# A hedgehog-attention and MoE kernel on one core: the quads of attention run as a software pipeline, with the matrix instructions in program order, the two MoE products mixed, and the tail loads made per batch

## The chip, the cores and the metric

The kernel runs on one core of a Trainium2 chip. The metric is the device time of one execution in microseconds; lower is better. The engines that matter are TensorE (PE in the profile; its weight loads are PEld), VectorE (DVE), ScalarE (ACT) and GpSimd (POOL). The sync engine (SP) only issues DMAs here.

## The reference, cut to what matters

```python
def phi(x):                              # q, k, v: batch 8, heads 8, 576 rows, 64 wide
    proj = einsum('bhsd,df->bhsf', x, w_phi)              # w_phi: 64 x 128
    proj = proj - max(abs(proj), axis=-1)
    return concatenate([exp(proj), exp(-proj)], axis=-1)
q_p, k_p = phi(q), phi(k)
kv  = einsum('bhsf,bhsd->bhfd', k_p, v)
num = einsum('bhsf,bhfd->bhsd', q_p, kv)
den = einsum('bhsf,bhf->bhs', q_p, sum(k_p, axis=2)) + 1e-6
x = (num / den), heads side by side                       # 4608 tokens x 512
h = x @ moe_w_in                                          # 512 x 2048
g = where(h > 0, h, exp(min(h, 0)) - 1)
out = g @ moe_w_out                                       # 2048 x 512
```

## The kernel before, in words

The attention is done in 16 quads: quad i holds four heads of batch i // 2. Of each head's 576 rows, 512 are the main part (four tiles of 128) and 64 are a tail; the tails of the four heads share tiles of their own (k_tails, q_tails, v_tails). The MoE is done in nine chunks of 512 tokens: one for each batch's main rows, and a ninth for all tails together.

The steps of a quad, with the names that the profile shows:

- transposes: PE turns k_main and q_main (tile tr, 16 products) and the tails (trt, 2) around, DVE copies them to kT and qT.
- k_head, five times (four heads and the tails): PE projects into pk, DVE takes the largest absolute value into m_k (the reduction), and ACT writes two exponentials (EK, or EKt for the tails). The exponentials wait for the reduction, because both read one bank of PSUM.
- k_scale: ACT makes em from m_k, and POOL multiplies v by it: four pieces of vs and two of vst.
- q_head, five times: the projection and the reduction into m_q alone. q_features: PE projects q again into pq, four times 512 wide and once for the tails, and ACT writes two exponentials of each (Eq, Eqt), then w from m_q.
- kv, twice: PE sums pkv over EK and vs (16 products of 65 columns and two of 130), ACT copies it to kv.
- out_head, four times, and out_tail: PE makes pn0 and pn1 from Eq and kv, DVE combines them into tot with two instructions (the tails into tott with four).
- divide: DVE makes den and rec, POOL multiplies tot by rec into x (four pieces) and xt.
- x_out: PE turns x around (eight products into tr and one into trt), DVE copies it to xT and xT_tail, the MoE's input.

An MoE chunk is 20 units. A unit of mm1 is four products of 512 columns into ph; then ACT makes e_sb, POOL u_sb and DVE gT. It is run 16 times. A unit of mm2 is 16 products of 512 columns into po; ACT copies it to o_sb and SP sends it off. It is run four times and reads all 16 pieces of gT.

Both halves take their PSUM from pools of four banks: apsum for everything of the attention (tag ap), mpsum for ph and po (tag mp). A tile of a pool waits until the last reader of the tile that held its bank is done.

In the program the steps of one quad follow each other, and the units of the batch before are dealt out between them: half of a batch's 20 units with each of the next two quads. The last batch and the tails' chunk (40 units) come after the last quad. That order is only a proposal: the framework's scheduler sets the order of the instructions on each engine when the program is built, by priorities and its own estimate of times. On the chip each engine then works through its list in order.

All loads with a change of type (q, k, the weights, the tails) are issued from POOL's list, among its computing instructions; v and the output go over SP.

Of the kernel before, what the change touches and what calls it, by code (L numbers as in the profile page):

```python
# [21 lines left out]
def kernel(  # L22
# [10 lines left out]
    nc = tc.nc  # L33
    P = 128
# [42 lines left out]
    w_in_r = moe_w_in.rearrange("(ct p) j -> p ct j", p=P)  # L77
# [3 lines left out]
    def load_w_in():  # L81
        for ct in range(N_CT):
            nc.gpsimd.dma_start(out=w_in_sb[:, ct, :], in_=w_in_r[:, ct, :])
# [16 lines left out]
    def load_tails(g0, g1):  # L100
        for src, dst, eng in (
            (k, k_tails, nc.gpsimd),
            (q, q_tails, nc.gpsimd),
            (v, v_tails, nc.gpsimd),
        ):
            flat = src.rearrange("b (g h) s d -> (b g) h s d", g=2)
            for s in range(2):
                for c in range(2):
                    eng.dma_start(
                        out=dst[s * TAIL:(s + 1) * TAIL, g0:g1, c, 0:D],  # L110
                        in_=flat[g0:g1, 2 * s + c, MAIN:S, :].rearrange(
                            "g j d -> j g d"
                        ),
                    )
# [40 lines left out]
    def attention_steps(i):  # L155
# [93 lines left out]
        def q_features(par, s):  # L249
            pq = apsum.tile([P, 4 * P], FP32, name="pq", tag="ap")  # L250
            nc.tensor.matmul(  # L251
                pq,
                w_phi_both[:, par, :],
                st["qT"][:, 4 * s:4 * s + 4, :].rearrange("p a b -> p (a b)"),
                start=True,
                stop=True,
            )
            for sg in range(2):
                nc.scalar.activation(  # L259
                    st["Eq"][:, par, s, sg, :], pq, ACT.Exp, scale=1.0 - 2.0 * sg  # L260
                )
# [22 lines left out]
        def kv(c):  # L284
# [12 lines left out]
            for s in range(2):  # L297
                for sg in range(2):
                    for t in range(NT):
                        nc.tensor.matmul(  # L300
                            pkv[:, s, sg, :],
                            st["EK"][:, 2 * s + c, sg, t * F:(t + 1) * F],
                            st["vs"][:, 2 * s + c, sg, t, :],
# [6 lines left out]
        def out_head(hh):  # L310
            s, c = divmod(hh, 2)
# [6 lines left out]
            for sg in range(2):  # L318
                pt = apsum.tile([P, NT, D1], FP32, name=f"pn{sg}", tag="ap")
                for t in range(NT):  # L320
                    tp, par = divmod(t, 2)
                    o = (2 * c + tp) * P
                    nc.tensor.matmul(  # L323
                        pt[:, t, :],
                        st["Eq"][:, par, s, sg, o:o + P],
# [39 lines left out]
        def divide():  # L365
# [9 lines left out]
            for hh in range(4):  # L375
                s, c = divmod(hh, 2)
# [52 lines left out]

# [112 lines left out]
```

## Time and profile before

| | |
|---|---|
| device time, two runs | 571.85 and 575.05 us, median 573.45 |
| the profiled execution | 574.21 us, of which the profile spans 572.4 |
| mean granted clock of PE | 0.901 |
| busy share of the span | PE 73%, DVE 51%, ACT 46%, POOL 46% |

The profile is of one execution. Busy time counts an instruction from its start to its end. Matmuls overlap, so their ends lie over the next one's start, and the distance of two starts says more than one's duration. Behind each row of a timeline stands, in square brackets, how long the engine had been idle ahead of it and what ended that. Lines are those of the kernel before; in the kernel after, the same lines stand one lower or so (L230 is L229 there).

### The profile page before, as it was taken

Reading aid. Unit: us, or ns where it says so; the run is one execution under the profiler, and the core shown is the slowest. Engines: PE = TensorE matmul, PEld = TensorE weight load, DVE = VectorE, ACT = ScalarE, POOL = GpSimd, SP = SyncE. Lnnn points to the kernel's source line nnn. Section 1 sums busy time; section 2 is a strip of 40 time slices with the busy share of each in tenths; the row PEclk is TensorE's granted clock in tenths of the full one; section 3 lists DMA queues with packets and bytes.
Section 4 is the critical chain, followed back from the end, with each engine's and each line's share of the span. In section 5 each row is a group of like instructions: output and inputs, shape, how many; then the busy total and the mean of one; then the engine's idle time right before and its main releaser. Section 6 shows DMA issues by size and latency. Waiting matters only on the chain.

```text
span 572.4 us, 8389 instructions
## 1 busy us (share of the span) xinstructions
PE 416.2 (73%) x3066; PEld 232.1 (41%) x3120; DVE 292.0 (51%) x647; ACT 264.8 (46%) x581; POOL 263.3 (46%) x392
## 2 busy tenths in 40 slices
PE   2302557768866786868787896778768867789996
PEld 1102334434443443434344444444435434444443
DVE  2300646484548435763576466836484538527070
ACT  1600244654374518371836265635655373725251
POOL 7637234654365426551556236633644265426060
PEclk9855767799989799999988998999799979899999
DMA  9999312122312215041403231323100100010103
GB/s 161 194 198 137 47 38 37 38 38 73 74 38 38 50 54 82 1 74 57 84 10 57 73 57 38 42 70 74 38 0 35 42 1 2 19 56 1 74 1 73
DMA packets 71496, 32.55 MB, mean 57 GB/s; under 512 B 47904, under 2 KB 66336, under 8 KB 71456
## 3 DMA queue, kind: packets, MB, share of 16 engines
q0 software_dynamic: 32416, 14.19, 21.7%
q1 hardware_dynamic: 39040, 17.83, 11.8%
q8 instruction: 24, 0.39, 0.3%
q14 instruction: 16, 0.13, 0.1%
HBM read 36.77 MB, written 9.44 MB: 81 GB/s over the span
## 4 chain that ended last, share of the span: by engine, by line
PE 31%; POOL 26%; issue 16%; DVE 11%; ACT 9%; DMA 6%; POOLq 0%; ACTq 0%; DVEq 0%
POOL vs L230 11%; PE po L459 11%; PE ph L438 10%; POOL x L377 6%; ACT EK L216 6%; DVE gT L451 4%; POOL vst L241 3%; DMA w_out_sb<-in_moe_w_out_dram 3%; PE tr L167 3%; POOL u_sb L448 3%; DVE tot L332 2%; DVE tot L338 2%; PE pkv L300 2%; PE pk L196 2%; DMA w_in_sb<-in_moe_w_in_dram 2%
## 5 line engine op out<-in xcount | busy, mean ns | idle before, releaser
L438 PE MATMUL ph<-xT,w_in_sb 128*128 128x512 bf16 x482 | 136.1, 394 | 18.0 <-DVE gT L451 16.1
L448 POOL TENSOR_SCALAR u_sb<-e_sb 128x512 bf16<-128x512 f32 x144 | 88.1, 619 | 116.9 <-ACT e_sb L446 105.7
L451 DVE SCALAR_TENSOR_TENSOR gT<-u_sb,ph 128x512 bf16<-128x512 bf16 x144 | 95.7, 681 | 86.5 <-POOL u_sb L448 85.7
L459 PE MATMUL po<-w_out_sb,gT 128*128 128x512 bf16 x554 | 138.9, 389 | 0.8
L446 ACT ACTIVATE e_sb<-ph 128x512 f32<-128x512 f32 x144 | 89.6, 636 | 102.6 <-PE ph L438 79.1
L438 PEld LDWEIGHTS <-w_in_sb 128*128 128x128 bf16 x576 | 55.6, 101 | 68.2 <-issue 31.0
L230 POOL TENSOR_TENSOR vs<-v_main,em 128x520 bf16<-128x520 f32 x64 | 65.7, 1056 | 36.3 <-ACT em L224 36.3
L377 POOL TENSOR_TENSOR x<-tot,rec 128x256 bf16<-128x256 f32 x64 | 37.2, 614 | 92.1 <-DVE rec L374 91.0
L459 PEld LDWEIGHTS <-gT 128*128 128x128 bf16 x576 | 55.4, 100 | 57.9 <-issue 4.2
L216 ACT ACTIVATE EK<-pk 128x512 bf16<-128x512 f32 x128 | 64.6, 633 | 24.3 <-DVE m_k L203 24.3
L467 ACT COPY o_sb<-po 128x512 f32<-128x512 f32 x36 | 21.1, 586 | 114.4 <-PE po L459 114.4
L332 DVE TENSOR_TENSOR tot<-pn,w 128x260 f32<-128x260 f32 x64 | 24.9, 424 | 93.1 <-PE pn L323 92.8
L259 ACT ACTIVATE Eq<-pq 128x512 bf16<-128x512 f32 x128 | 67.6, 712 | 4.7 <-PE pq L251 4.7
L289 PE MATMUL pkv<-vst,EKt 128*128 128x130 bf16 x64 | 11.2, 271 | 72.8 <-POOL vst L241 52.7
L203 DVE TENSOR_REDUCE m_q<-pk 128x4 f32<-128x512 f32 (+1 forms) x80 | 48.4, 634 | 10.0 <-PE pk L196 9.0
L203 DVE TENSOR_REDUCE m_k<-pk 128x4 f32<-128x512 f32 (+1 forms) x80 | 46.4, 630 | 2.8 <-PE pk L196 2.5
L289 PEld LDWEIGHTS <-EKt 128*128 128x128 bf16 x64 | 6.7, 108 | 80.1 <-issue 69.6
L308 ACT CAST kv<-pkv 128x260 bf16<-128x260 f32 x32 | 12.0, 376 | 57.1 <-PE pkv L300 57.1
L196 PE MATMUL pk<-w_phi_both,qT 128*128 128x256 bf16 x144 | 28.1, 301 | 13.0 <-ACT EK L216 11.3
L394 PE MATMUL tr<-ident,x 128*128 128x128 bf16 x128 | 13.5, 232 | 24.9 <-POOL x L377 24.9
L401 DVE COPY xT<-tr 128x1024 bf16<-128x1024 bf16 x16 | 11.1, 692 | 39.2 <-PE tr L394 39.2
L196 PE MATMUL pk<-w_phi_both,kT 128*128 128x256 bf16 x144 | 25.0, 287 | 7.4 <-ACT EK L216 6.5
(61 smaller groups left out, 473.0 us busy)
## 6 DMA issues: line engine op xcount, KB each, us to landing
v_main<-in_v_dram SPq DMA_DIRECT2D x64, 128.0 KB, 2.6
out_dram<-o_sb SPq DMA_DIRECT2D x32, 256.0 KB, 2.3
k_main<-in_k_dram POOLq DMA_DIRECT2D x16, 256.0 KB, 4.4
q_main<-in_q_dram POOLq DMA_DIRECT2D x16, 256.0 KB, 4.9
w_in_sb<-in_moe_w_in_dram POOLq DMA_DIRECT2D x4, 512.0 KB, 9.6
w_out_sb<-in_moe_w_out_dram POOLq DMA_DIRECT2D x4, 512.0 KB, 17.3
out_dram<-o_sb SPq DMA_DIRECT2D x8, 128.0 KB, 2.3
k_tails<-in_k_dram POOLq DMA_DIRECT2D x4, 96.0 KB, 13.8
```

Of the source, the lines that this page charges most:

```text
L196: nc.tensor.matmul(pk[:, 2 * j:2 * j + 2, :].rearrange("p a b -> p (a b)"), xT[:, 2 * hh + j, :], w_phi_rhs, start=True, stop=True,)
L203: nc.vector.tensor_reduce(m[:, 4 * hh:4 * hh + 2 * n], pk[:, 0:2 * n, :], axis=AX.X, op=ALU.max, apply_absolute_value=True,)
L216: nc.scalar.activation(dst, pk, ACT.Exp, scale=1.0 - 2.0 * sg)
L230: nc.gpsimd.tensor_tensor(vs[:, hh], vb[:, hh:hh + 1].to_broadcast((P, 2, NT, D1)), em[:, :, 4 * hh:4 * hh + 4, None].to_broadcast((P, 2, ...
L259: nc.scalar.activation(st["Eq"][:, par, s, sg, :], pq, ACT.Exp, scale=1.0 - 2.0 * sg)
L332: nc.vector.tensor_tensor(tot, pn[1], st["w"][:, 4 * hh:4 * hh + 4, None].to_broadcast((P, NT, D1)), op=ALU.mult,)
L377: nc.gpsimd.tensor_tensor(st["x"][:, s, :, c, :], st["tot"][:, hh, :, 0:D], rec[:, 4 * hh:4 * hh + 4, None].to_broadcast((P, NT, D)), op=A ...
L438: nc.tensor.matmul(ph, w_in_sb[:, ct, jt * P:(jt + 1) * P], xTs[ch][:, ct, :], start=(ct == 0), stop=(ct == N_CT - 1),)
L446: nc.scalar.activation(e_sb, ph, ACT.Exp)
L448: nc.gpsimd.tensor_scalar(u_sb, e_sb, -1.0, 1.0, op0=ALU.add, op1=ALU.mult)
L451: nc.vector.scalar_tensor_tensor(gTs[ch][:, jt, :], u_sb, 0.0, ph, op0=ALU.min, op1=ALU.max)
L459: nc.tensor.matmul(po, gT[:, jt, tt * P:(tt + 1) * P], w_out_sb[:, jt, :], start=(jt == 0), stop=(jt == N_JT - 1),)
```

## The change

Seven things are done.

1. The program's order of steps is written in slots. Slot n holds the k steps, k_scale, the q steps and q_features of quad n, together with kv, out and x of quad n - 1; kv and out alternate with the k steps on PE. The transposes of quad n + 1 end the slot. There are 17 slots (0 to 16).
2. PE's instructions are held in program order; the scheduler still orders the other engines.
3. The units of MoE chunk c are mixed: after every fourth mm1 of chunk c stands one mm2 of chunk c - 1. Batch 0's chunk has no mm2 beside it, and four mm2 of the last chunk are left for the end.
4. The units are dealt out a slot later: 8 (all mm1) in each of the slots 3 and 4, 10 (eight mm1, two mm2) in each of the slots 5 to 16, none ahead. What stands behind slot 16 is 32 units of mm1 and 12 of mm2.
5. The tails of q, k and v are loaded per batch, with six DMAs of 64 x 4 runs each: one batch at the start, the next after every second slot. Before, there were 12 such DMAs for quads 0 to 3 and then 12 with three times as many runs for the rest.
6. w_out is loaded after slot 1 in the program, behind w_in; w_in comes in eight pieces of 64 partitions, not four of 128.
7. The heads of a quad are paired otherwise (c and s change places throughout, and the rows of w_in with them). The instructions and their sizes stay the same.

```diff
     w_phi_rhs = w_phi_both.rearrange("p a b -> p (a b)")
     w_in_sb = consts.tile([P, N_CT, DFF], BF16)
-    w_in_r = moe_w_in.rearrange("(ct p) j -> p ct j", p=P)
+    w_in_r = moe_w_in.rearrange("(g c s d) j -> g c s d j", g=2, c=2, s=2)
     w_out_sb = consts.tile([P, N_JT, DM], BF16)
     w_out_r = moe_w_out.rearrange("(jt p) o -> p jt o", p=P)
     def load_w_in():
         for ct in range(N_CT):
-            nc.gpsimd.dma_start(out=w_in_sb[:, ct, :], in_=w_in_r[:, ct, :])
+            for c in range(2):
+                nc.gpsimd.dma_start(
+                    out=w_in_sb[c * D:(c + 1) * D, ct, :],
+                    in_=w_in_r[ct // 2, c, ct % 2],
+                )
     def load_w_out():
         for jt in range(0, N_JT, 4):
@@ -97,21 +101,16 @@
     v_tails = consts.tile([P, NQ, 2, D1], BF16)
     nc.vector.memset(v_tails[:, :, :, D:D1], 1.0)
-    def load_tails(g0, g1):
-        for src, dst, eng in (
-            (k, k_tails, nc.gpsimd),
-            (q, q_tails, nc.gpsimd),
-            (v, v_tails, nc.gpsimd),
-        ):
-            flat = src.rearrange("b (g h) s d -> (b g) h s d", g=2)
+    def load_tails(b):
+        for src, dst in ((k, k_tails), (q, q_tails), (v, v_tails)):
+            heads = src[b].rearrange("(gc s) j d -> s j gc d", s=2)
             for s in range(2):
-                for c in range(2):
-                    eng.dma_start(
-                        out=dst[s * TAIL:(s + 1) * TAIL, g0:g1, c, 0:D],
-                        in_=flat[g0:g1, 2 * s + c, MAIN:S, :].rearrange(
-                            "g j d -> j g d"
-                        ),
-                    )
+                nc.gpsimd.dma_start(
+                    out=dst[s * TAIL:(s + 1) * TAIL, 2 * b:2 * b + 2, :, 0:D].rearrange(
+                        "p g c d -> p (g c) d"
+                    ),
+                    in_=heads[s, MAIN:S],
+                )
     NV = 3
@@ -246,18 +245,18 @@
                 )
             st["vs"], st["vst"] = vs, vst
-        def q_features(par, s):
+        def q_features(par, c):
             pq = apsum.tile([P, 4 * P], FP32, name="pq", tag="ap")
...
@@ -415,17 +414,18 @@
         def each(f, *a):
             return lambda: f(*a)
-        return (
-            [transposes]
-            + [each(k_head, hh) for hh in range(5)]
-            + [k_scale]
-            + [each(q_head, hh) for hh in range(5)]
-            + [each(q_features, par, s) for s in range(2) for par in range(2)]
-            + [q_features_tail]
-            + [each(kv, c) for c in range(2)]
-            + [each(out_head, hh) for hh in range(4)]
-            + [out_tail, divide, x_out]
-        )
+        return {
+            "tr": [transposes],
+            "k": [each(k_head, hh) for hh in range(5)],
+            "scale": [k_scale],
+            "q": [each(q_head, hh) for hh in range(5)],
+            "qf": [each(q_features, par, c) for c in range(2) for par in range(2)]
+            + [q_features_tail],
+            "kv": [each(kv, c) for c in range(2)],
+            "out": [each(out_head, hh) for hh in range(4)]
+            + [lambda: (out_tail(), divide())],
+            "x": [x_out],
+        }
     gTs = {}
@@ -476,39 +476,86 @@
                     in_=o_sb[e * TAIL:(e + 1) * TAIL, :],
                 )
-    def moe_units(ch):
-        return [lambda jt=jt: mm1(ch, jt) for jt in range(N_JT)] + [
-            lambda tt=tt: mm2(ch, tt) for tt in range(CHUNK // P)
-        ]
+    def slot_steps(n):
+        new = attention_steps(n) if n < NQ else None
+        old = quads.get(n - 1)
+        nxt = []
+        steps = []
+        k = new["k"] if new else [None] * 5
+        qs = new["q"] if new else [None] * 5
+        if old:
+            steps += [old["kv"][0], k[0], old["kv"][1], k[1]]
+            for hh in range(3):
+                steps += [old["out"][hh], k[2 + hh]]
+            steps += [old["out"][3], new and new["scale"][0], old["out"][4]]
+        else:
+            steps += k + new["scale"]
+        steps += qs
+        if old:
+            steps += old["x"]
+        if new:
+            steps += new["qf"]
+            quads[n] = new
+        if n + 1 < NQ:
+            steps.append(lambda: transpose_next(n + 1))
+        return [f for f in steps if f]
+    quads = {}
+    ready = {}
+    def transpose_next(n):
+        ready[n] = build_steps(n)
+        ready[n]["tr"][0]()
+    build_steps = attention_steps
+    def attention_steps(n):
+        return ready.pop(n)
+    def mixed_units(ch):
+        units = []
+        for jt in range(N_JT):
+            units.append(lambda jt=jt: mm1(ch, jt))
+            if ch > 0 and jt % 4 == 3:
+                units.append(lambda tt=jt // 4: mm2(ch - 1, tt))
+        return units
+    ctx.enter_context(tc.manual_schedule(engines={mybir.EngineType.PE}))
     load_quad(0)
-    load_tails(0, 4)
+    load_tails(0)
     load_quad(1)
     load_w_in()
     load_quad(2)
-    load_w_out()
-    load_tails(4, NQ)
+    transpose_next(0)
     pending = []
-    for i in range(NQ):
-        b, qd = divmod(i, 2)
-        steps = attention_steps(i)
-        share = len(pending) if qd == 1 else len(pending) // 2
+    for n in range(NQ + 1):
+        steps = slot_steps(n)
+        share = len(pending) // 2 if n % 2 == 1 else len(pending)
         done = 0
-        for n, step in enumerate(steps):
+        for j, step in enumerate(steps):
             step()
-            upto = share * (n + 1) // len(steps)
+            upto = share * (j + 1) // len(steps)
             while done < upto:
                 pending.pop(0)()
                 done += 1
-        if i + 3 < NQ:
-            load_quad(i + 3)
-        if qd == 1:
-            pending.extend(moe_units(b))
-    pending.extend(moe_units(B))
-    for unit in pending:
+        if n == 1:
+            load_w_out()
+        if n + 3 < NQ:
+            load_quad(n + 3)
+        if n % 2 == 0 and n // 2 + 1 < B:
+            load_tails(n // 2 + 1)
+        if n > 0 and n % 2 == 0:
+            pending.extend(mixed_units(n // 2 - 1))
+    for unit in pending + mixed_units(B):
         unit()
+    for tt in range(CHUNK // P):
+        mm2(B, tt)
 # ---- launch: one core; inputs and outputs as the reference has them ----
```

The numbers of instructions that compute are unchanged on each engine. Three places show how they move.

The first is POOL at the start, from the loads of w_in to the first k_scale (vs and vst, quad 0). Before:

```order
L83 DMA w_in_sb<-in_moe_w_in_dram 128x2048 x4
L137 DMA k_main<-in_k_dram 128x4x256
L137 DMA q_main<-in_q_dram 128x4x256
L87 DMA w_out_sb<-in_moe_w_out_dram 128x4x512 x4
L109 DMA k_tails<-in_k_dram 64x12x64 x4
L109 DMA q_tails<-in_q_dram 64x12x64 x4
L109 DMA v_tails<-in_v_dram 64x12x64 x4
L230 TENSOR_TENSOR vs<-v_main_98,em 128x520 x4
L241 TENSOR_TENSOR vst_104<-v_tails,em 64x4x65 x2
```

Now:

```order
L84 DMA w_in_sb<-in_moe_w_in_dram 64x2048 x8
L136 DMA k_main<-in_k_dram 128x4x256
L136 DMA q_main<-in_q_dram 128x4x256
L229 TENSOR_TENSOR vs<-v_main_98,em 128x520 x4
L240 TENSOR_TENSOR vst_104<-v_tails,em 64x4x65 x2
```

Of the 18 DMAs between the w_in pieces and vs, two are left; w_out and the tails now come behind vst.

The second is the same engine between x of quad 0 and the next scale behind it, which was that of quad 1 and now is that of quad 2 (slot 2). Before, two loads stood there:

```order
L377 TENSOR_TENSOR x<-tot,rec 128x4x64 x4
L383 TENSOR_TENSOR xt<-tott,rec 128x128
L137 DMA k_main<-in_k_dram 128x4x256
L137 DMA q_main<-in_q_dram 128x4x256
L230 TENSOR_TENSOR vs<-v_main_100,em 128x520 x4
```

Now the place ends with these rows:

```order
L108 DMA k_tails<-in_k_dram 64x4x64 x2
L108 DMA q_tails<-in_q_dram 64x4x64 x2
L108 DMA v_tails<-in_v_dram 64x4x64 x2
L229 TENSOR_TENSOR vs<-v_main_102,em 128x520 x4
L240 TENSOR_TENSOR vst_104<-v_tails,em 64x4x65 x2
L108 DMA k_tails<-in_k_dram 64x4x64 x2
```

The loads of the tails of all later batches have no buffer to wait for, and the scheduler has drawn them together: 18 of them stand between x of quad 0 and the scale of quad 2 (with four loads of k and q), 18 more between that scale and the first u_sb of slot 3. After that there are none.

The third is a quad in the middle of the run, on POOL. Before, two quads differ; the one with most u_sb between scale and x and the other:

```order
L230 TENSOR_TENSOR vs<-v_main_102,em 128x520 x4
L241 TENSOR_TENSOR vst_104<-v_tails,em 64x4x65 x2
L448 TENSOR_SCALAR u_sb<-e_sb 128x512 x10
L377 TENSOR_TENSOR x<-tot,rec 128x4x64 x4
L383 TENSOR_TENSOR xt<-tott,rec 128x128
L448 TENSOR_SCALAR u_sb<-e_sb 128x512 x2
L137 DMA k_main<-in_k_dram 128x4x256
L137 DMA q_main<-in_q_dram 128x4x256
L448 TENSOR_SCALAR u_sb<-e_sb 128x512
L230 TENSOR_TENSOR vs<-v_main_98,em 128x520 x4
```

Now every slot from 7 on has this (the five u_sb are one of the slot before and four of this one):

```order
L448 TENSOR_SCALAR u_sb<-e_sb 128x512 x5
L229 TENSOR_TENSOR vs<-v_main_98,em 128x520 x4
L240 TENSOR_TENSOR vst_106<-v_tails,em 64x4x65 x2
L376 TENSOR_TENSOR x<-tot,rec 128x4x64 x4
L382 TENSOR_TENSOR xt<-tott,rec 128x128
L448 TENSOR_SCALAR u_sb<-e_sb 128x512 x3
L136 DMA k_main<-in_k_dram 128x4x256
L136 DMA q_main<-in_q_dram 128x4x256
```

The scale of the new quad now stands straight ahead of x of the old one, and three u_sb stand behind xt. On DVE, the part of the slot behind rec reads:

```order
L373 RECIPROCAL rec<-den 128x18
L202 TENSOR_REDUCE m_q<-pk 128x4 x4
L451 SCALAR_TENSOR_TENSOR gT<-u_sb,ph 128x512
L202 TENSOR_REDUCE m_q<-pk 128x2
L451 SCALAR_TENSOR_TENSOR gT<-u_sb,ph 128x512
L400 COPY xT<-tr 128x1024
L410 COPY xT_tail<-trt 128x2x64
L451 SCALAR_TENSOR_TENSOR gT<-u_sb,ph 128x512
L171 COPY kT<-tr 128x1024
L171 COPY qT<-tr 128x1024
```

where before it was:

```order
L374 RECIPROCAL rec<-den 128x18
L401 COPY xT<-tr 128x1024
L411 COPY xT_tail<-trt 128x2x64
L172 COPY kT<-tr 128x1024
L172 COPY qT<-tr 128x1024
```

Two gT, which need u_sb, now stand ahead of the copy of xT.

More of the change, by code (lines that the diff above doesn't have):

```diff
@@ L259, in q_features @@
                 nc.scalar.activation(
-                    st["Eq"][:, par, s, sg, :], pq, ACT.Exp, scale=1.0 - 2.0 * sg
+                    st["Eq"][:, par, c, sg, :], pq, ACT.Exp, scale=1.0 - 2.0 * sg
                 )
@@ L301, in kv @@
                             pkv[:, s, sg, :],
-                            st["EK"][:, 2 * s + c, sg, t * F:(t + 1) * F],
-                            st["vs"][:, 2 * s + c, sg, t, :],
+                            st["EK"][:, 2 * c + s, sg, t * F:(t + 1) * F],
+                            st["vs"][:, 2 * c + s, sg, t, :],
                             start=False,
@@ L310, in out_head @@
         def out_head(hh):
-            s, c = divmod(hh, 2)
+            c, s = divmod(hh, 2)
             if hh == 0:
@@ L375, in divide @@
             for hh in range(4):
-                s, c = divmod(hh, 2)
+                c, s = divmod(hh, 2)
                 nc.gpsimd.tensor_tensor(
```

6 lines of the change are left out of this document (3 added, 3 removed).

## The prediction

> **What bounds the kernel now.** I read the table of stretches first: the time from the first kv to the last product of quad 15's slot, and the MoE work that is left behind it. (Behind the stretch and its length stand the busy time and instructions of PE, PEld, DVE, ACT and POOL, then PE's granted clock.)
>
> ```profile
> 512.58:567.90 55.32, 55.06 (x252) 24.96 (x255) 21.93 (x32) 23.79 (x40) 19.79 (x32) 1.00 0.13 39
> 52.88:512.58 459.70, 352.30 (x2773) 202.15 (x2822) 261.26 (x594) 229.61 (x516) 210.21 (x308) 0.91 0.23 46
> ```
>
> The end is bound by PE: 256 products (252 recorded) in 55.32 us, 0.216 each. The 459.7 us ahead of it are bound by no engine: PE is busy 352.3 (22.0 per quad), DVE 261.3. What bounds them is order, so next comes the chain that ended last: x appears in it once per quad, and ten quads apart (the fence leaves out nine) it stands 299.95 us later, **30.0 us a quad**.
>
> ```profile
> 206.37 2.34 POOL x L377 x4
> ...
> 506.32 2.34 POOL x L377 x4
> ```
>
> Then the timeline of the start.
>
> ```profile
> 18.91 0.34 ACT L224 ACTIVATE em<-m_k 128x18 f32<-128x18 f32 x2
> ...
> 30.00 0.75 POOL L109 DMA_DIRECT2D k_tails<-in_k_dram  x1 [1.66 <-DMA w_in_sb<-in_moe_w_in_dram]
> ...
> 45.20 2.25 POOL L109 DMA_DIRECT2D v_tails<-in_v_dram  x3 [0.63 <-issue]
> 47.44 4.11 POOL L230 TENSOR_TENSOR vs<-v_main,em 128x520 bf16<-128x520 f32 x4
> 51.51 1.32 POOL L241 TENSOR_TENSOR vst<-v_tails,em 64x260 bf16<-64x260 bf16 x2
> 52.88 0.38 PE L289 MATMUL pkv<-vst,EKt 128*128 128x130 bf16 x2 [31.32 <-POOL vst L241]
> ```
>
> em is there at 19.25, but POOL takes up vs at 47.44: it is issuing loads, and each waits for an earlier load to land. PE loses 31.3 us there.
>
> **Term 1, the start.** Only k and q of quad 2 now stand between w_in and vs. If no wait remains, vs starts at em, 19.25, and kv at 19.3 + 4.1 + 1.3 = 24.7. If POOL waits for the last piece of w_in (30.00 + 0.75), kv starts at 36.2. There are six tail DMAs less ahead, so I take 26.5, nearer to the first: **-26.4** against 52.9.
>
> **Term 2, the full slots (5 to 15).** I walk one slot with the durations of now; they are the groups of the page and rows of one quad.
>
> ```profile
> L448 POOL TENSOR_SCALAR u_sb<-e_sb 128x512 bf16<-128x512 f32 x144 | 88.1, 619 | 116.9 <-ACT e_sb L446 105.7
> L451 DVE SCALAR_TENSOR_TENSOR gT<-u_sb,ph 128x512 bf16<-128x512 bf16 x144 | 95.7, 681 | 86.5 <-POOL u_sb L448 85.7
> ...
> L332 DVE TENSOR_TENSOR tot<-pn,w 128x260 f32<-128x260 f32 x64 | 24.9, 424 | 93.1 <-PE pn L323 92.8
> ...
> L203 DVE TENSOR_REDUCE m_k<-pk 128x4 f32<-128x512 f32 (+1 forms) x80 | 46.4, 630 | 2.8 <-PE pk L196 2.5
> ```
>
> ```profile
> 328.00 0.40 POOL L383 TENSOR_TENSOR xt<-tott,rec 128x128 bf16<-128x128 f32 x1
> ...
> 328.53 0.69 DVE L401 COPY xT<-tr 128x1024 bf16<-128x1024 bf16 x1 [2.90 <-PE tr L394]
> 328.73 3.40 PE L459 MATMUL po<-w_out_sb,gT 128*128 128x512 bf16 x15
> ...
> 339.04 0.75 ACT L216 ACTIVATE EKt<-pk 128x256 bf16<-128x256 f32 x2
> ...
> 340.04 0.43 ACT L224 ACTIVATE em<-m_k 128x18 f32<-128x18 f32 x2
> 340.95 4.10 POOL L230 TENSOR_TENSOR vs<-v_main,em 128x520 bf16<-128x520 f32 x4
> ...
> 342.64 3.22 ACT L259 ACTIVATE Eq<-pq 128x512 bf16<-128x512 f32 x6
> ...
> 345.01 1.31 POOL L241 TENSOR_TENSOR vst<-v_tails,em 64x260 bf16<-64x260 bf16 x2
> ...
> 346.38 0.38 PE L289 MATMUL pkv<-vst,EKt 128*128 128x130 bf16 x2 [3.27 <-ACT e_sb L446]
> ...
> 346.55 1.08 PE L300 MATMUL pkv<-vs,EK 128*128 128x65 bf16 x16
> ```
>
> Zero is the start of kv. (a) *To em.* The first reduction can start at about 1.6 (16 products of kv, 1.1, then pk). Up to the last, DVE has five reductions (2.9), six tot (2.5) and three gT (2.0), 7.4 us, in an order that makes it wait some 1.9 more: pk of the second head stands behind the second kv and a unit of mm1 on PE (1.5), and two gT come behind u_sb (0.4). So the reductions end at 10.9, and EKt (0.75) and em (0.4) end at **12.0**. (b) *To xt.* POOL's list has vs, vst, x, xt in a row: 4.1 + 1.3 + 2.35 + 0.4 = **8.15**, to 20.15. rec is there earlier, and PE, with a mm2 and the q steps in between, at about 17.7; it then waits for x. (c) *To the next kv.* Ahead of the copy of xT, DVE has two gT and a reduction, and the first gT needs a u_sb that stands behind xt: 0.62 + 0.68 + 0.42 + 0.68 + 0.69 = 3.1, and pq number four needs the bank that this copy frees. Then a unit of mm1 (0.87) and pq of the tails: the transposes start at 4.5 and take 0.9; ACT, with 0.54 per Eq, is as late. DVE copies kT (0.69), the tails' transpose follows at 5.9, and the second mm2 (16 x 0.216 = 3.45) ends at **9.45**. The sum is 12.0 + 8.15 + 9.45 = **29.6 us**, against 30.0 now: little of what PE waits goes away, since em, the scale and x stand in one line through POOL, and the Eq follow it. Eleven slots are 325.6.
>
> Bounds of a slot: if the 1.9 of (a) and the 0.5 or so of DVE's queue in (c) don't show, 27.2; if each of some 20 hand-offs takes 0.1 more than I counted (rows start 0.05 to 0.1 after their releaser), 31.6.
>
> **Term 3, the other slots.** Slots 1 and 2 have no MoE. The same walk without gT and mm2 gives 22.3; I take 24, since PE has little work there and its clock may be low (below). In slot 2, 18 tail DMAs and four loads stand on POOL ahead of the scale. At 0.75 a piece, as in the row of v_tails (three in 2.25), they are 16.5 us behind x and hold the scale 3 back: 27. In slot 3, 18 more hold the first u_sb, and with it DVE's gT, some 3.5 back: 26 + 3.5 (a full slot less the last mm2 is 26). Slot 4: 26. Slot 16 has no quad of its own: PE's work is 64 x 0.216 + some 4 of kv, out and x = 18, with waits 20. Together 24 + 27 + 29.5 + 26 + 20 = 126.5. With 325.6 that is 452.1, against 459.7 now: **-7.6**.
>
> **Term 4, the end.** Behind the last slot stand 44 units, 32 x 4 + 12 x 16 = 320 products, not 256: 64 x 0.216 = **+13.8**. The 4.4 us behind the last product stay.
>
> **Terms at nothing.** The new pairing of heads changes no instruction. The four issues more for w_in (0.6 each) lie in POOL's wait for em; without that cover term 1 is 2.4 less, inside its bounds. The four of w_out (3.0) lie ahead of em of quad 1, or at worst in front of x of quad 0, and w_out lands long before slot 5. Loads issued late in a slot (k, q) are for three slots on.
>
> **The sum.** -26.4 - 7.6 + 13.8 = -20.2 on 572.4: a span of 552.2. The profiled execution took 574.21, 0.76 above the median of 573.45, so I forecast 573.45 - 20.2, **553 us** (-3.5%).
>
> **The rivals.** *PE comes up to its load.* If the waits of (a) and (c) overlap better than my walk lets them, a slot nears PE's 22.0. For it speaks that kv, out, k and mm1 are now all ready together; against it, that 8.15 of POOL between em and xt stay serial. At 24.5: 553 - 11 x 5.1 = 497. Chance 0.17.
>
> *The hand-offs are longer*, slots of 31 to 32.5: 553 + 11 x 1.4 to 2.9 = 568 to 585. Chance 0.13.
>
> *The loads don't come per batch.* The list shows the tails drawn together, so what the start gives may be taken back in slots 2 and 3. The late tails now take 2.4 each with their wait (0.75 + 1.66 in the row at 30.00), with three times the runs and beside w_out. If half of the 36 took 1.7 more and half of that were hidden: +15, 568. Against: the last three v_tails took 0.75. Chance 0.10.
>
> *PE's clock falls in every slot.* This is the case on the slower side. The stretches behind two waits of now, and the second wait (the first, of 3.27, is the row at 346.38):
>
> ```profile
> 345.00:348.00 3.00, 1.45 (x19) 1.25 (x19) 0.93 (x2) 2.33 (x7) 2.84 (x6) 0.68 0.41 92
> ...
> 375.00:378.00 3.00, 2.95 (x55) 2.17 (x53) 0.96 (x2) 1.34 (x3) 0.31 (x1) 1.00 0.15 34
> ```
>
> ```profile
> 374.65 0.28 PE L289 MATMUL pkv<-vst,EKt 128*128 128x130 bf16 x2 [3.00 <-POOL vst L241]
> ```
>
> Behind the wait of 3.27 us the clock granted is 0.68; behind the one of 3.00 it stays at 1.00. My wait for x is 17.7 to 20.15, 2.4 us. From some 3.1 on, 0.7 more, each slot has 0.7 us of wait and 3 us of PE's work at half clock (3.0 more): 553 + 11 x 3.7 = 594. Chance 0.06, because the wait is broken by x's first four transposes. The Trainium skill says the same more sharply ("TensorE: Matmul & The Clock Gate", What's actually happening: an idle window of about 3.4 us halves the clock, and the window runs free), by which this case needs waits of that size; the trace agrees about, with 0.68 behind 3.27 us.
>
> A second rule speaks against the many small loads: the Trainium skill ("DMA: Bandwidth & Descriptors", Anatomy of one DMA) fits a DMA from POOL's queue with 2.0 us and the bytes on top. Back to back, the 28 more DMAs of POOL would be some 56 us by an estimate from that fit; the three v_tails issued in 2.25 us speak against their being serial.
>
> **How the numbers follow.** The likeliest case has 0.50 and by itself goes from 540 to 566 (slots 28.5 to 30.8); the rivals have 0.17, 0.13, 0.10 and 0.06, and 0.04 stays for what I don't see. The range takes the slots' bounds: 553 - 11 x 2.4 = 527, and 4 less for the start and slots 3 and 4, 522; 553 + 11 x 2.0 = 575, and 5 of the late-start bound, 580. Below the range lies most of the first rival, above it the clock. About 2% (11.5 us) is what a measurement of this kernel can tell from no change: below 562 are most of the likeliest (0.44), the first rival and some of the unseen, 0.64; above 585 the clock and the unseen, 0.08; 0.28 stays.
>
> **What would show it.** Right: kv starts at 25 to 29 us; x stands 29 to 30.5 apart in slots 6 to 15, with PE waiting for x on POOL each time; POOL full of L108 up to some 80 us; 69 us of products at the end at clock 1.00. Wrong: x 27 or less apart with PE above 85% busy (first rival), a clock below 0.85 in the full slots (the clock), or a first kv behind 36.

## The result, and the profile after

The changed kernel takes **538.77 us** (538.64 and 538.91, two runs) against 573.45: a ratio of 0.9406, with a 95% interval of 0.9322 to 0.9489, or 34.7 us less. The forecast was 553, in a range of 522 to 580: the direction holds and the mechanism mostly too, and 14 us of the gain were not seen ahead. The time lies just below the 540 to 566 that the likeliest case had by itself. The profiled execution took 538.64, its span is 536.5.

The table of stretches of after, from the first kv to the first product behind the last slot, and from there to the last product (columns as in the prediction):

```profile
26.65:462.83 436.18, 330.98 (x2700) 189.21 (x2740) 274.36 (x590) 231.29 (x512) 239.67 (x354) 0.92 0.33 56
462.83:531.90 69.07, 68.75 (x315) 31.22 (x319) 22.01 (x32) 26.15 (x44) 19.83 (x32) 1.00 0.14 46
```

So of the 35.9 us between the spans the start gives 26.2 (52.88 to 26.65), the slots give 23.5 (459.70 to 436.18), and the end takes 13.7 back (55.32 to 69.07). The start, on the timeline:

```profile
18.10 0.41 ACT L223 ACTIVATE em<-m_k 128x18 f32<-128x18 f32 x2
...
20.45 0.76 POOL L136 DMA_DIRECT2D q_main<-in_q_dram  x1 [0.55 <-DMA w_in_sb<-in_moe_w_in_dram]
...
21.22 4.09 POOL L229 TENSOR_TENSOR vs<-v_main,em 128x520 bf16<-128x520 f32 x4
25.29 1.31 POOL L240 TENSOR_TENSOR vst<-v_tails,em 64x260 bf16<-64x260 bf16 x2
26.65 0.38 PE L288 MATMUL pkv<-vst,EKt 128*128 128x130 bf16 x2 [3.76 <-POOL vst L240]
```

PE's wait for vst is 3.8 us, where it was 31.3. em is there at 18.51, and POOL is still 2.7 us with the loads of k and q, the last of which waits for a piece of w_in. The chain that ended last shows a regular slot; eight of them lie between these two pieces (those between are left out):

```profile
173.27 4.11 POOL vs L229 x4
...
395.19 4.11 POOL vs L229 x4
```

That is 221.92 / 8 = **27.7 us a slot**. Before it was 30.0, the forecast was 29.6. One slot on the timeline, from kv to kv:

```profile
273.39 0.28 PE L288 MATMUL pkv<-vst,EKt 128*128 128x130 bf16 x2
273.51 0.68 PE L299 MATMUL pkv<-vs,EK 128*128 128x65 bf16 x16
274.45 0.69 DVE L202 TENSOR_REDUCE m_k<-pk 128x4 f32<-128x512 f32 x1 [2.16 <-PE pk L195]
...
280.28 0.40 PE L322 MATMUL pn<-kv,Eq 128*128 128x65 bf16 x8 [1.01 <-DVE tot L331]
...
282.34 0.41 DVE L202 TENSOR_REDUCE m_k<-pk 128x2 f32<-128x256 f32 x1
283.45 0.34 ACT L223 ACTIVATE em<-m_k 128x18 f32<-128x18 f32 x2
283.88 4.11 POOL L229 TENSOR_TENSOR vs<-v_main,em 128x520 bf16<-128x520 f32 x4
...
289.33 2.33 POOL L376 TENSOR_TENSOR x<-tot,rec 128x256 bf16<-128x256 f32 x4
291.14 0.40 PE L393 MATMUL tr<-ident,x 128*128 128x128 bf16 x4 [1.57 <-POOL x L376]
291.62 0.40 POOL L382 TENSOR_TENSOR xt<-tott,rec 128x128 bf16<-128x128 f32 x1
297.59 3.62 PE L459 MATMUL po<-w_out_sb,gT 128*128 128x512 bf16 x16
301.05 0.28 PE L288 MATMUL pkv<-vst,EKt 128*128 128x130 bf16 x2
```

The three parts of the prediction's walk can be read off it: (a) to em, 273.39 to 283.79, is 10.4; (b) em to the end of xt, at 292.02, is 8.2; (c) to the next kv is 9.0. PE waits for x, and while it does, program order holds everything behind x. In (c) the 16 products at 297.59 stand as one block between the transposes and kv.

### The profile page after: what moved, and what is told of

The parts are those of the page before. It is cut to its first block, busy times and chain, and to the rows that moved or that the text cites. A ratio compares the mean times of both kernels' runs of the same rounds, so it can differ in the third digit from the quotient of the medians.

```text
span 536.5 us, 8427 instructions
## 1 busy us (share of the span) xinstructions
PE 410.2 (76%) x3073; PEld 226.5 (42%) x3120; DVE 306.8 (57%) x647; ACT 268.8 (50%) x581; POOL 279.2 (52%) x420
## 4 chain that ended last, share of the span: by engine, by line
POOL 34%; PE 26%; issue 19%; DVE 9%; DMA 7%; ACT 4%; POOLq 0%; ACTq 0%
POOL vs L229 11%; PE ph L438 11%; PE po L459 10%; POOL x L376 6%; POOL u_sb L448 6%; DMA q_main<-in_q_dram 6%; DVE gT L451 4%; POOL vst L240 3%; DVE m_k L202 1%; ACT EKt L215 1%; POOL q_main L136 1%; DMA w_in_sb<-in_moe_w_in_dram 1%; ACT e_sb L446 1%; PE pq L250 1%; PE tr L393 1%
## 5 line engine op out<-in xcount | busy, mean ns | idle before, releaser
L438 PE MATMUL ph<-xT,w_in_sb 128*128 128x512 bf16 x482 | 128.2, 390 | 1.9 <-issue 0.4
L459 PE MATMUL po<-w_out_sb,gT 128*128 128x512 bf16 x560 | 128.1, 381 | 0.9
L215 ACT ACTIVATE EK<-pk 128x512 bf16<-128x512 f32 x128 | 68.9, 602 | 23.3 <-DVE m_k L202 23.2
L202 DVE TENSOR_REDUCE m_k<-pk 128x4 f32<-128x512 f32 (+1 forms) x80 | 50.3, 633 | 41.3 <-PE pk L195 40.8
L322 PE MATMUL pn<-kv,Eq 128*128 128x65 bf16 x512 | 30.0, 196 | 18.9 <-DVE tot L331 14.9
L322 PEld LDWEIGHTS <-Eq 128*128 128x128 bf16 x512 | 26.1, 99 | 32.6 <-issue 26.2
L393 PEld LDWEIGHTS <-x 128*128 128x128 bf16 x128 | 8.4, 108 | 66.9 <-POOL x L376 66.9
L195 PE MATMUL pk<-w_phi_both,kT 128*128 128x256 bf16 x144 | 29.9, 286 | 8.6 <-DVE tot L337 6.2
L250 PE MATMUL pq<-qT,w_phi_both 128*128 128x512 bf16 x64 | 25.2, 464 | 8.2 <-DVE xT L400 5.0
L331 DVE TENSOR_TENSOR tot<-pn,w 128x260 f32<-128x260 f32 x64 | 26.9, 420 | 3.0 <-PE pn L322 2.1
L337 DVE TENSOR_TENSOR tot<-tot,pn 128x260 f32<-128x260 f32 x64 | 26.7, 418 | 0.7
```

What stands on the lines that cost most here:

```text
L202: nc.vector.tensor_reduce(m[:, 4 * hh:4 * hh + 2 * n], pk[:, 0:2 * n, :], axis=AX.X, op=ALU.max, apply_absolute_value=True,)
L215: nc.scalar.activation(dst, pk, ACT.Exp, scale=1.0 - 2.0 * sg)
L250: nc.tensor.matmul(pq, w_phi_both[:, par, :], st["qT"][:, 4 * c:4 * c + 4, :].rearrange("p a b -> p (a b)"), start=True, stop=True,)
L322: nc.tensor.matmul(pt[:, t, :], st["Eq"][:, par, c, sg, o:o + P], st["kv"][:, c, s, sg, :], start=True, stop=True,)
L438: nc.tensor.matmul(ph, w_in_sb[:, ct, jt * P:(jt + 1) * P], xTs[ch][:, ct, :], start=(ct == 0), stop=(ct == N_CT - 1),)
L459: nc.tensor.matmul(po, gT[:, jt, tt * P:(tt + 1) * P], w_out_sb[:, jt, :], start=(jt == 0), stop=(jt == N_JT - 1),)
```

## The experiments

All ratios are to the kernel before, which took 572.0 to 573.9 us beside these runs.

### Where the gain came from: the start

**The later loads alone, in the kernel before.**

```diff
-    load_w_out()
-    load_tails(4, NQ)
     (in the loop, behind the steps of quad i)
+        if i == 0:
+            load_w_out()
+        if i == 1:
+            load_tails(4, NQ)
```

> The kernel before with one part of the change: w_out and the late tail loads are issued behind the first scale on POOL, all else as it was. Theory (the start is a gain of its own): the first kv at 27 to 30 us instead of 52.9, some of it given back while the late tails hold POOL ahead of the scale of quad 1; 548 to 562 us, most likely 555. Rival (the loads only change places, the loads take the same time out of quads 0 to 3): 566 or more. Distance of two x in the middle of the run 30.0 as before, by both.

Measured: 549.95 us, ratio 0.9631 (0.9581 to 0.9681). The first vs starts at 19.46, and x of quad 15 is still 24.7 us earlier than before (481.61, not 506.32). This alone is 22.7 of the 34.7 us.

**The changed kernel without its start.**

```diff
     load_quad(2)
+    load_w_out()
+    for b in range(1, B):
+        load_tails(b)
     (and the loads of w_out and of the tails in the loop are gone)
```

> The changed kernel with the start undone: w_out and the tails of all batches are issued right behind the loads of quad 2, so ahead of the first scale on POOL. Theory: the first kv at 55 to 62 us, 29 to 35 later than in the changed kernel, with 5 to 6 us got back in slots 2 and 3, which lose their tail loads; 562 to 570 us. Rival (the start is worth less in the pipeline, because slots 1 to 3 catch up): 550 or less. Slots 5 to 15 at 27.65 by both.

Measured: 569.79, ratio 0.9964 (0.9943 to 0.9985). In the list of waits of this run the wait that had gone is back, and longer:

```profile
PE pkv L288 <- POOL vst L240: 45.7, 1, 45.7
```

So with all loads first, the pipeline over quads, the program order and the mixing gain 2 to 3 us together (0.9 to 3.3 by the interval, less than 2%). They gain more than that inside: with 48 tail transfers on POOL ahead of it, not 24, the first kv of this run comes at 68.31, later than the 55 to 62 expected and 15.4 us later than before, and the slots make up for it. Against after, the start is worth 31.0 us.

### What the program order costs

**The same kernel, and PE's order left to the scheduler.**

```diff
-    ctx.enter_context(tc.manual_schedule(engines={mybir.EngineType.PE}))
```

> The changed kernel with PE's order left to the scheduler, so with the slots, mixing and loads but without program order on PE. Theory (program order is no source of the gain; the line through POOL is the same): 530 to 548 us, a slot 27 to 28.5. Rival (holding PE in program order is what makes slots shorter than 30): 555 or more.

Measured: **507.5, ratio 0.8882 (0.8847 to 0.8918)**. Both theories fail: holding PE in program order costs 31 us, and the gain of the rest is there without it. Between x of quad 5 and of quad 14 slots take 25.8 us ((402.16 - 170.31) / 9). This mean hides two lengths that take turns, 24.9 and 26.5 us; two slots from kv to kv in the table of stretches (PE's granted clock is the third figure from the end):

```profile
283.41:308.30 24.89, 22.29 (x188) 12.46 (x187) 18.32 (x40) 15.92 (x35) 15.04 (x23) 1.00 0.36 66
308.30:334.77 26.47, 23.87 (x189) 13.03 (x188) 18.67 (x40) 16.02 (x35) 12.80 (x19) 0.94 0.28 58
```

The longer ones have a lowered clock behind the wait for x. At full clock program order costs 2.8 us a slot (27.7 for 24.9), and the lowered clock takes a part of this back. PE's rows from x to the next kv, in a slot at full clock of this run:

```profile
301.28 0.40 PE L393 MATMUL tr<-ident,x 128*128 128x128 bf16 x4 [2.22 <-POOL x L376]
301.85 0.40 PE L393 MATMUL tr<-ident,x 128*128 128x128 bf16 x4 [0.17 <-POOL x L376]
302.20 0.23 PE L405 MATMUL trt<-ident,xt 128*128 128x128 bf16 x1
302.26 0.38 PE L250 MATMUL pq<-qT,w_phi_both 128*128 128x512 bf16 x1
302.48 0.38 PE L438 MATMUL ph<-xT,w_in_sb 128*128 128x512 bf16 x1
...
303.13 0.81 PE L459 MATMUL po<-w_out_sb,gT 128*128 128x512 bf16 x3
...
304.43 0.59 PE L459 MATMUL po<-w_out_sb,gT 128*128 128x512 bf16 x2
...
306.36 2.10 PE L459 MATMUL po<-w_out_sb,gT 128*128 128x512 bf16 x9
308.30 0.28 PE L288 MATMUL pkv<-vst,EKt 128*128 128x130 bf16 x2
```

The wait for x is still there (2.2 us), but behind it stand single MoE products in the gaps between pq and the transposes, and 9 of them ahead of kv, not 16. From the end of xt to kv it is 6.2 us, not 9.0; in the next slot, with the lowered clock, it is 7.7. The line that was taken out speaks of PE alone; the scheduler then also set the other engines' lists differently, so the 31 us are those of both together.

**The same line put into the kernel before.**

```diff
+    ctx.enter_context(tc.manual_schedule(engines={mybir.EngineType.PE}))
```

> The kernel before with TensorE's instructions held in program order, nothing else changed. Theory (program order by itself costs, because a product that could be issued in a wait stands behind the waiting instruction): 590 us or more. Rival (the order of TensorE is neutral, and what the scheduler's order gains in the changed kernel belongs to its slots): 565 to 580.

Measured: 607.37, ratio 1.0606 (1.0580 to 1.0632), 35 us slower. The cost of program order belongs to neither kernel in particular. A part of the 35 us may be the clock: its mean is 0.87 to 0.89, and that of the kernel before 0.90 to 0.91 beside it.

**Program order with smaller pieces.**

```diff
-    def mm2(ch, tt):
+    def mm2(ch, tt, parts=(0, 1, 2, 3)):   (four products to a part)
-            if ch > 0 and jt % 4 == 3:
-                units.append(lambda tt=jt // 4: mm2(ch - 1, tt))
+            if ch > 0:
+                units.append(lambda jt=jt: mm2(ch - 1, jt // 4, (jt % 4,)))
```

> The changed kernel with program order kept, but each down-projection of 16 products cut into four pieces of 4, one piece behind each up-projection. Theory (what program order costs is its grain: the piece of 16 stands whole behind or ahead of a wait): slots of 26.5 us or less, 515 to 528. Rival (program order itself costs, whatever the grain, as no piece can move into a wait that was not foreseen): 533 to 542.

Measured: 534.55, ratio 0.9336 (0.9314 to 0.9359). The time is that of the rival: smaller pieces bring 4 us of the 31. A slot is still 27.4 (x at 179.28 and at 398.46, eight slots). But the two runs differ in the clock as well. The full slots of this run are at 0.94 and less, one of them here, and most of after's are at 1.00:

```profile
217.22:244.41 27.19, 23.20 (x188) 13.22 (x187) 18.27 (x39) 16.05 (x36) 14.33 (x22) 0.94 0.29 59
```

So the finer grain may be worth more than the 4 us show; no run here has it at full clock. On POOL's timeline of this run the finer units also break up the line from em to x:

```profile
281.36 3.09 POOL L229 TENSOR_TENSOR vs<-v_main,em 128x520 bf16<-128x520 f32 x3 [1.21 <-ACT em L223]
284.42 0.61 POOL L448 TENSOR_SCALAR u_sb<-e_sb 128x512 bf16<-128x512 f32 x1
...
287.99 2.32 POOL L376 TENSOR_TENSOR x<-tot,rec 128x256 bf16<-128x256 f32 x4
```

x starts 6.6 us behind vs, not 5.5 as in after.

**Program order with the wait for x filled by hand.**

```diff
-        if old:
-            steps += old["x"]
         if new:
             steps += new["qf"]
             quads[n] = new
+        if old:
+            steps += old["x"]
```

> The changed kernel, program order kept, with the transposes of x behind the next quad's q feature products instead of ahead of them: TensorE has 10 products and more to do in the 1.7 us in which it waits for x. Theory (program order costs where a wait was foreseen wrongly, and the wait for x is the largest of these): 12 to 16 waits of 1.7 us and the two long ones shorter, 505 to 520. Rival (the slot is a line over all engines, the transposes of x reach VectorE and the next products later, and the wait turns up elsewhere): 530 to 545.

Measured: 528.18, ratio 0.9255 (0.9216 to 0.9295), 10.6 us less than after: between the two expectations. The profiled execution took 531.14, 7.5 less than that of after, and 5.2 of this is there by x of quad 4 (145.40, not 150.61); from quad 5 to quad 14 a slot is 27.4 ((420.87 - 174.26) / 9), 0.4 less than in after over the same quads. The waits of this run say why:

```profile
PE pq L250 <- DVE m_q L202: 38.3, 17, 4.9
PE tr L393 <- POOL x L376: 12.2, 3, 5.8
```

In after, PE waits 55.0 us for x. Now it waits 12.2 for x, and 38.3 for the reductions that free the bank of pq. Filled by hand, most of the wait turned up again a few instructions further on.

**The same move in the scheduler's order** (with bulk tail loads, below).

> The scheduler's order with the bulk tail loads (500.4), and the transposes of x behind the q feature products. Theory (a wait that was foreseen wrongly costs there too): 478 to 492. Rival (the scheduler's order fills the wait with products already, so the place of x matters little): 496 to 506.

Measured: **472.67, ratio 0.8276 (0.8244 to 0.8308)**, 27.7 less than without the move and less than the theory allowed. Slots are 24.3 us ((369.21 - 150.69) / 9), all at a clock of 1.00; without the move they are 24.9 at full clock and 26.5 with the lowered one. Of the 27.7 us, 13.4 are there by x of quad 5 (150.69, not 164.12). Behind it five of nine slots have the lowered clock without the move and none with it: by an estimate from these figures that is 8 us (5 x 1.6). Program order against the scheduler's in the table of stretches, from x of quad 5 to x of quad 14, first the run before this one, then this one:

```profile
174.26:420.87 246.61, 196.15 (x1659) 115.26 (x1684) 164.91 (x350) 143.01 (x317) 125.37 (x184) 1.00 0.22 47
```

```profile
150.69:369.21 218.52, 198.32 (x1655) 112.45 (x1681) 162.95 (x350) 140.12 (x315) 124.70 (x184) 1.00 0.25 52
```

PE has the same work at the same clock; its idle time falls from 50.5 to 20.2 us in nine slots. The run before this one also has the tail loads per batch, which lie ahead of these slots.

### What binds a slot

**x on VectorE.**

```diff
-                nc.gpsimd.tensor_tensor(     (x, and the same for xt)
+                nc.vector.tensor_tensor(
```

> The changed kernel with x and xt (the division) done by DVE instead of POOL. Theory (a slot is set by the line em, vs, vst, x, xt on POOL and what follows it): PE's wait for x falls from about 1.7 us a slot to near 0, a slot from 27.65 to 24.7 to 26, in all 508 to 522 us, though DVE has 1.5 to 2 us more to do in each slot. Rival (DVE or PE is full in effect, POOL's line is only where the wait shows): 533 or more.

Measured: 546.22, ratio 0.9558 (0.9511 to 0.9606), 7 us slower than after. The theory fails. On the timeline of this run:

```profile
319.90 3.13 DVE L376 TENSOR_TENSOR x<-tot,rec 128x256 bf16<-128x256 f32 x4
323.27 2.48 DVE L202 TENSOR_REDUCE m_q<-pk 128x4 f32<-128x512 f32 x4
324.02 0.37 PE L195 MATMUL pk<-w_phi_both,qT 128*128 128x256 bf16 x1 [2.90 <-DVE m_q L202]
```

x holds up the reductions, and PE waits 2.9 us for the first of them. POOL's line was not alone; DVE's list is right behind it. Two more things in this run keep it from showing how much each is worth. Behind the wait the granted clock is 0.50 (from 324.00 to 327.00); it falls so in every slot from 6 to 14, to 0.94 over the slot, and a slot is 29.0 us. And x takes 3.13 us here, beside vs and vst on POOL; where POOL computes nothing beside it, it takes less than half:

```profile
439.17 1.42 DVE L376 TENSOR_TENSOR x<-tot,rec 128x256 bf16<-128x256 f32 x4
```

**x on both** (on the scheduler's order with bulk tail loads).

```diff
-                nc.gpsimd.tensor_tensor(     (x alone)
+                (nc.gpsimd, nc.vector)[c].tensor_tensor(
```

> The scheduler's order with the bulk tail loads (500.4), and two of the four divisions by the denominators on VectorE, the other two and the tails' on GpSimd as before. Theory (the line to x still sets the slot there: TensorE waits 2.2 us for x in each, and the split takes 1.2 us of GpSimd's 2.3): 483 to 492. Rival (VectorE's list then holds the next quad's reductions, as it did when all of x was on it): 497 to 510.

Measured: 485.85, ratio 0.8501 (0.8469 to 0.8533), 14.5 less than without the split. A slot is 25.0 us ((384.54 - 159.34) / 9), not 25.8. Two pieces on POOL (1.18) and two on DVE (1.32) run partly side by side. At full clock this shortens a slot by 0.3 us only, from 24.9; the rest is that the clock is lowered in one slot of three here, not in about every second one:

```profile
242.96:267.56 24.60, 22.22 (x185) 12.46 (x187) 19.30 (x41) 15.80 (x35) 13.56 (x19) 1.00 0.33 65
267.56:293.43 25.87, 23.55 (x185) 12.91 (x187) 19.30 (x41) 16.01 (x35) 13.56 (x19) 0.93 0.32 63
```

So the time came out as the theory had it, but this does not show that the line to x sets the slot.

**x later and on both.**

> Both edits on the scheduler's order with the bulk tail loads: the transposes of x behind the q feature products, and x divided by GpSimd and VectorE. Theory (with x later, the line to x is off TensorE's path, so the split has nothing left to take): 468 to 476, as with x later alone (472.7). Rival (the two gains add, 14.5 and 27.7): 456 to 464.

Measured: **466.95, ratio 0.8153 (0.8117 to 0.8189)**, the fastest kernel of the study. The split still brings 5.7 us, a little more than the theory allowed and far from the 14.5 of the rival: the gains overlap. A slot is 23.8 us (x at 150.05 and at 364.15, nine slots). In this run and the one without the split these slots are all at a clock of 1.00, so the 0.5 us a slot are the split's own.

### Mixing and the tail loads

**MoE units as before** (on the scheduler's order).

```diff
-        for jt in range(N_JT):
-            units.append(lambda jt=jt: mm1(ch, jt))
-            if ch > 0 and jt % 4 == 3:
-                units.append(lambda tt=jt // 4: mm2(ch - 1, tt))
+        units = [lambda jt=jt: mm1(ch, jt) for jt in range(N_JT)]
+        units += [lambda tt=tt: mm2(ch, tt) for tt in range(CHUNK // P)]
-    for tt in range(CHUNK // P):
-        mm2(B, tt)
```

> The changed kernel in the scheduler's order, with the MoE units of a batch in the order of before: 16 up-projections and then the 4 down-projections of the same batch, so that none is left for the end but the last batch's and the tails'. Theory (mixing only moves 64 products to the end, which are not hidden there): 492 to 500, from 507.5, with 256 products at the end in place of 320. Rival (mixing keeps the slots even, and without it the slots with the four down-projections in a row grow by as much): 505 to 515.

Measured: 514.86, ratio 0.8990 (0.8962 to 0.9018), 7.4 slower than mixed. The rival holds. From the last x to the end it is 9.6 us less (443.94 to 513.5, not 426.44 to 505.6), but the last x comes 17.5 later: without mixing one slot of two has 10 units of four products and the other 6 such and four of 16, so 40 products and 88, and slots swing between 24.5 and 29.5 (vs at 169.90, 199.38 and 223.85). 5.1 of the 17.5 are there by x of quad 5 (175.36, not 170.31), by which this run has done the 64 products that mixing leaves for the end; the other 12.4 come in slots that hold the same number of products on average. Mixing pays the 64 products at the end with even slots.

**Six tail transfers in place of 36** (on the scheduler's order).

```diff
-        if n % 2 == 0 and n // 2 + 1 < B:
-            load_tails(n // 2 + 1)
+        if n == 0:
+            load_tails(1, 2)
+        if n == 1:
+            load_tails(2, B)      (batches 2 to 7 in one DMA for each half of k, q and v)
```

> The changed kernel in the scheduler's order, with the tail rows of batches 2 to 7 in 6 transfers behind slot 1 in place of 36 behind slots 2 to 12. Theory (the small tail transfers hold GpSimd's list in slots 2 and 3, ahead of the value scaling): 500 to 504, from 507.5. Rival (the wait is the transfers' bytes or is hidden, and the bulk load only moves it): 506 to 512.

Measured: 500.37, ratio 0.8739 (0.8701 to 0.8778), 7 us less, as the theory had it. On POOL's timeline the vs of quad 2 comes 4.0 us earlier; first with 36, then with six transfers:

```profile
63.27 1.26 POOL L108 DMA_DIRECT2D v_tails<-in_v_dram  x2
64.48 0.67 POOL L108 DMA_DIRECT2D k_tails<-in_k_dram  x1
65.10 4.15 POOL L229 TENSOR_TENSOR vs<-v_main,em 128x520 bf16<-128x520 f32 x4
```

```profile
52.45 1.96 POOL L108 DMA_DIRECT2D v_tails<-in_v_dram  x2
61.10 4.09 POOL L229 TENSOR_TENSOR vs<-v_main,em 128x520 bf16<-128x520 f32 x4 [6.69 <-ACT em L223]
```

In the second vs waits for em, not for POOL; x of quad 3 is 6.4 us ahead (114.36, not 120.80).

## Why the prediction was right, and where it was wrong

**Term 1, the start: right.** -26.4 forecast, -26.2 measured, and two runs show the cause from both sides: the loads alone take 22.7 us off the kernel before, and undoing them puts 31.0 on the kernel after. That it fits to 0.2 us is partly luck: 26.5 was chosen between 24.7 and 36.2 without a count of the 2.7 us that POOL still spends with loads behind em.

**Term 2, the full slots: the mechanism right, the size wrong.** The line em, vs, vst, x, xt through POOL is there (8.2, forecast 8.15), PE waits for x in every slot (it comes there 16.2 us behind kv and waits 1.6, where I had 17.7 and 2.4), and (c) is 9.0 for 9.45. The mis-sized step is (a), 10.4 where I had 12.0. The first reduction starts at 1.06 behind kv, not 1.6: I took kv from a row of before whose 16 products last 1.08 at a clock of 0.68, and in after the row lasts 0.68 us, at full clock. From there to the end of the last reduction it is 8.3, not 9.3: DVE waits 1.3 us in it, not the 1.9 that I put in for PE's order and u_sb, and its 14 instructions, whose rows sum to 7.7, fill only 7.0, because most start before the row ahead of them ends. Over slots 5 to 15 (134.67 to 438.33, 303.7 us for 325.6) this and (c) are 21.9 us, more than all of the error, as term 3 goes the other way. My lower bound for the slot, 27.2, named these waits; I judged them to stay. So the sign that I had given for being right, x 29 to 30.5 us apart, did not come: it is 27.7, and the slot is near that bound. The first rival's sign, 27 or less with PE above 85% busy, did not come either.

**Term 3: too short.** Slots 1 to 4 took 25.8, 26.9, 28.9 and 26.5, 108.0 for a forecast of 106.5. In slots 2 and 3 POOL was at the tail loads until 86 us, where some 80 were forecast. Slot 16 took 24.5, not 20: with little PE work, the wait for x is 4.9 us and the products behind it run at half clock (0.50 granted from 456.40 to 459.40).

```profile
455.41 1.18 PE L393 MATMUL tr<-ident,x 128*128 128x128 bf16 x8 [4.94 <-POOL x L376]
456.49 1.91 PE L438 MATMUL ph<-xT,w_in_sb 128*128 128x512 bf16 x4
```

**Term 4, the end: right.** 69.07 us for 320 products, +13.8, at clock 1.00.

**The sum.** The slots' -7.6 became -23.5: -21.9 more in the full slots, +1.5 in slots 1 to 4, +4.5 in slot 16. With -26.2 for the start, +13.7 for the end and 0.1 more behind it, that is -35.9.

**What the steps left out.** I walked the slot with program order as given and asked only what it makes wait; I never priced the other order, which the kernel before had. At 31 us it is as large as the start, and it works against the change. A price for it could have been sought in before's timeline, where the scheduler puts single products of mm1 between the outputs of the heads, while DVE works on them:

```profile
351.91 0.28 PE L323 MATMUL pn<-kv,Eq 128*128 128x65 bf16 x4
352.03 0.38 PE L438 MATMUL ph<-xT,w_in_sb 128*128 128x512 bf16 x1
352.25 0.28 PE L323 MATMUL pn<-kv,Eq 128*128 128x65 bf16 x4
```

At the same place in after PE stands still for 1.0 us (the row at 280.28), with four products to a unit and no way to take one ahead.

**The rivals.** PE did not come up to its load in after (180.3 of 221.9 us between quads 5 and 13), but it nearly did once program order was gone and x moved. The loads per batch did cost what the third rival named, on a smaller scale: 7 us, measured in the scheduler's order. The clock rival came up in two of eleven slots of after. Behind waits of the same length, the table of stretches shows:

```profile
291.00:294.00 3.00, 2.35 (x16) 1.19 (x17) 1.37 (x3) 1.45 (x3) 2.18 (x5) 1.00 0.00 0
...
152.50:155.50 3.00, 2.83 (x14) 1.21 (x15) 1.59 (x4) 1.09 (x2) 1.96 (x4) 0.65 0.00 0
319.00:322.00 3.00, 2.77 (x16) 1.11 (x14) 1.71 (x4) 1.69 (x4) 1.84 (x4) 0.77 0.02 5
```

Those two slots took 28.1 and 28.4 us for the usual 27.7, so 0.5 to 0.7 each, not the 3.7 of the forecast. In the variants it came up more often: in every full slot with smaller pieces, in nearly every one with x on VectorE, and in about every second one in the scheduler's order, where it costs 1.6 us. By the Trainium skill ("TensorE: Matmul & The Clock Gate", What's actually happening) it takes an idle window of about 3.4 us, and the window runs free. That some slots are hit and most are not fits a free window; that a wait of 1.6 us with 0.2 behind it is enough does not fit 3.4 us of idle time, and the measurement decides. Beside the two waits only x's transposes run in the 2.6 us up to pq (150.86 to 153.42); whether these count as idle, no run here shows.

**What stays open.** How much of the 31 us is PE's own order and how much the other engines' lists, which changed with it, was not separated. The variants differ in how often the clock falls, as well as in what their edits aim at, and no run holds the clock fixed; so what the smaller pieces, the split of x and the later x are worth by themselves is known only as far as the slots at full clock show it. The new pairing of heads and the halves of w_in were not tried by themselves.

## What to carry to other kernels

Price a change's parts against each other, not only against the kernel before: here the later loads, the pipeline and the mixing gained 65 us, and holding one engine to the written order gave 31 of them back. Work that depends on little, such as MoE products, is worth most where it can stand in any gap one product at a time; to put a piece by hand into the wait that one sees got 11 of the 31 us back under program order, and most of the wait moved to the next dependence. And look at the clock of each slot before a variant's time is put down to its edit: of two variants, one can have the lowered clock in every slot and the other in none. Last, take a duration from a row at the clock that the changed kernel will have.

## What the hardware showed that was not expected

The same four divisions took 2.33 us on POOL. On DVE they took 3.13 in the slots 5 to 14, beside vs and vst on POOL, and 1.42 or 1.43 in the five places where POOL computed nothing beside them (the one at 439.17 is shown). vst took 1.56 beside them, and 1.31 in after. So what such an instruction takes on one of these two engines depended on what the other did at the time. And a lowered clock, 0.65 and 0.77, was seen behind waits of no more than 1.6 us. The length of a wait alone does not decide it: with x later under program order PE waits 2.6 us ahead of pq in each of the slots 6 to 14 and the clock stays at 1.00 over all of them, while in the scheduler's order a wait of 2.2 us has the lowered clock behind it in one slot and not in the next.
